# Sliding-window attention by groups of 64 queries with one window of 128 keys each, values copied on chip

## The chip, the cores and the metric

One core of one Trainium2 chip. The metric is the device time of one execution in microseconds. Experiments e2 to e5 ran on one chip and e6 to e8 on another, each set with the kernel before in the same rounds: it took 341.51 us (median) with the first set and 340.94 with the second, at best 340.80 and 340.67. Engine names are the profile's: PE is TensorE's matmul, PEld its weight load, DVE is VectorE, ACT is ScalarE, POOL is GpSimd, SP is SyncE.

## The reference, cut to what matters

```python
# q, k, v: (8 batches, 8 heads, 576 positions, 64)
scores = q @ k.T / 8                       # masked: 0 <= i - j < 64
attn = softmax(scores)                     # each query sees at most 64 keys
x = (attn @ v) -> (4608 tokens, 512)
out = (relu(x @ w_gate) * (x @ w_val)) @ w_out      # d_ff = 1536
```

## The kernel before

The attention is done in 24 units of 192 queries (all heads), three for each batch. Two units make a tile of 384 tokens, whose FFN follows: 96 `h` matmuls over gate and value, then 36 `op` matmuls. (`h` is the hidden layer, `g_sb` the product of its two halves, `op` the output; `st` are the scores, `p` their exp.) One instruction stream for PE weaves the two together. A small Python scheduler decides the order while the program is built: every piece of work advances a model clock by its estimated length, and attention steps are queued at planned times T on that clock.

```python
def at(self, t, fn): heapq.heappush(self.heap, (t, self.n, fn)); ...
def pop(self):
    _, _, fn = heapq.heappop(self.heap)
    self.clock += fn() or 0.0              # a step returns its estimate in us
def advance(self, t):                      # called between FFN matmul groups
    while self.heap and self.heap[0][0] <= max(t, self.clock): self.pop()
...
def u_st(u, hhs=(0, 1)):                   # scores, keys on partitions
    for hh in hhs:
        for w in range(2):                 # two windows of 128 keys x 128 queries
            for dh in range(2):
                for g in range(G):         # four row groups side by side
                    nc.tensor.matmul(d["st"][hh][g][:, c:c + 128], kT[...128 keys], qT[...128 queries], ...)
    return 0.65
def u_pv_wide(u):                          # units 2 to 23
    for c in (0, 2, 1, 3):
        for e in range(2):
            for w in range(2):
                nc.tensor.matmul(d["pv"][...][..., 64 * w:64 * w + 128], v16[:, w, ...], d["p"][...128], ...)
    return 0.9
...
def plan_unit(u, T, exp=0.8, mask=1.5, pv=3.9, ...):
    if u > 5: W.at(T - 17, lambda: v_load(u))
    W.at(T, lambda: u_st(u))
    ...                                    # exp and mask of the four head groups, copy, sum, norm
    W.at(T + pv, lambda: u_pv(u))
...
for t in range(3, NU // 2):                # two units a tile
    ...                                    # the batch's k and q
    plan_unit(2 * t, T + ...)
    plan_unit(2 * t + 1, T + 13.2, ...)
    T += 26.525
...
for t in range(2, NU // 2):
    ready(2 * t + 2)                       # emit everything up to this tile's xt
    hidden(t, 0, TT)                       # 96 h matmuls
    output(t)                              # 36 op matmuls
```

The end of a unit is a chain on DVE: PV result, four transposes of the sums (`sT`), reciprocal (`rT`), transpose back (`rs`), the product `xt`. The FFN of a tile waits for its second unit's `xt`. A new batch's k and q are transposed on DVE too (`kT`, `qT`).

The softmax here doesn't subtract the row's maximum and nothing guards it: scores larger than these inputs give would overflow.

## Time and profile before

| | before |
|---|---|
| median (all runs at first) | 340.94 us (340.88 to 341.48) |
| profiled span, granted clock | 339.0 us, 0.999 |
| PE busy | 98% |
| DVE, ACT busy | 74%, 55% |

A group's line reads: source line, engine, operation, written tile <- read tiles, shapes, count, then busy us and mean ns of one, then the idle time just before and who ended it. A line of the chain of waits reads: start, length, what.

### The profile page before, as it was taken

The numbers are of one execution on the slowest core, as the hardware profiler recorded it, in microseconds if no ns is written. First come the engines' busy times: TensorE is split into PE (matmuls) and PEld (weight loads), VectorE is DVE, ScalarE is ACT, GpSimd is POOL, SyncE is SP. The second block draws the span as 40 slices with busy tenths as digits, with TensorE's granted clock in tenths as the row PEclk, the third lists the DMA queues.
The fourth block names the chain that finished last, engine by engine and source line by source line (L and its number), as shares of the span: only waits on it lengthen the run. The fifth ranks groups of instructions, "written<-read, shape, count | busy, mean of one in ns | idle before, by whom it ended". The sixth has DMA issues, their size and how long they took to land.

```text
span 339.0 us, 7368 instructions
## 1 busy us (share of the span) xinstructions
PE 331.4 (98%) x2954; PEld 201.0 (59%) x2954; DVE 251.9 (74%) x452; ACT 186.1 (55%) x383; POOL 65.6 (19%) x99
## 2 busy tenths in 40 slices
PE   8899999999999999999999999999999999999996
PEld 4576496856546646646556555555655664664653
DVE  5777969997989748797798783888878963974430
ACT  4657166746736637638546556565565663663322
POOL 8723421411204004021021310420120200000000
PEclk9999999999999999999999999999999999999999
DMA  8999999980374854962251951972324402001002
GB/s 216 177 207 196 203 189 170 134 132 7 20 123 31 143 85 54 151 93 41 16 64 64 151 75 63 121 87 90 24 19 106 34 2 93 2 2 63 31 2 94
DMA packets 59666, 30.29 MB, mean 89 GB/s; under 512 B 46064, under 2 KB 51056, under 8 KB 59632
## 3 DMA queue, kind: packets, MB, share of 16 engines
q0 software_dynamic: 53872, 19.21, 51.8%
q1 hardware_dynamic: 5616, 10.55, 8.5%
q8 instruction: 23, 0.38, 0.5%
q14 instruction: 11, 0.09, 0.1%
q10 hardware_dynamic: 144, 0.07, 0.1%
HBM read 39.58 MB, written 9.44 MB: 145 GB/s over the span
## 4 chain that ended last, share of the span: by engine, by line
PE 85%; DVE 10%; issue 3%; ACT 1%; ACTq 0%
PE h L412 50%; PE op L426 21%; PE pv L305 6%; PE st L246 3%; DVE sT L335 3%; PE st L213 2%; DVE g_sb L400 2%; DVE qT L184 1%; DVE xt L350 1%; DVE p L266 1%; DVE kT L184 1%; PE op L458 1%; ACT p L260 1%; DVE rs L344 1%; PE st L206 1%
## 5 line engine op out<-in xcount | busy, mean ns | idle before, releaser
L412 PE MATMUL h<-xt,wg 128*128 128x384 f16 (+1 forms) x640 | 116.5, 310 | 0.7 <-DVE xt L350 0.7
L412 PE MATMUL h<-xt,wv 128*128 128x384 f16 (+1 forms) x640 | 116.4, 310 | 0.0
L400 DVE TENSOR_TENSOR g_sb<-r_sb,h 128x384 f16<-128x384 f32 x144 | 78.1, 549 | 50.3 <-PE h L412 48.3
L397 ACT ACTIVATE r_sb<-h 128x384 f32<-128x384 f32 x144 | 71.1, 495 | 52.0 <-PE h L412 43.4
L426 PE MATMUL op<-wo,g_sb 128*128 128x512 f16 x420 | 93.0, 379 | 0.0
L412 PEld LDWEIGHTS <-wg 128*128 128x128 f16 x640 | 59.3, 98 | 34.7 <-DVE xt L350 1.4
L412 PEld LDWEIGHTS <-wv 128*128 128x128 f16 x640 | 59.7, 98 | 31.6
L192 POOL DMA_DIRECT2D v<-in_v_dram x48 | 40.4, 846 | 185.7 <-PE pv L305 166.3
L426 PEld LDWEIGHTS <-g_sb 128*128 128x128 f16 x420 | 40.9, 98 | 47.9 <-DVE g_sb L400 0.4
L335 DVE STREAM_TRANSPOSE sT<-pv 64x384 f32<-64x384 f32 x88 | 51.1, 580 | 11.3 <-PE pv L305 9.8
L260 ACT ACTIVATE p<-st 128x512 f16<-128x512 f32 x92 | 49.9, 606 | 10.4 <-PE st L246 10.3
L433 ACT COPY o_sb<-op 128x512 f32<-128x512 f32 x35 | 20.5, 585 | 60.6 <-PE op L426 60.5
L323 ACT COPY xv<-pv 64x384 f32<-64x384 f32 x88 | 41.6, 473 | 17.6 <-DVE sT L335 8.5
L266 DVE TENSOR_TENSOR p<-p,mask 128x512 f16<-128x512 f16 x88 | 34.4, 419 | 7.0 <-ACT p L260 6.3
L305 PE MATMUL pv<-p,v 128*128 128x128 f16 x352 | 24.1, 219 | 0.4 <-DVE p L266 0.3
L344 DVE STREAM_TRANSPOSE rs<-rT 128x768 f32<-128x768 f32 x24 | 23.5, 978 | 0.8
L305 PEld LDWEIGHTS <-v 128*128 128x128 f16 x352 | 21.6, 98 | 3.7 <-issue 0.6
L350 DVE TENSOR_TENSOR xt<-xv,rs 128x768 f16<-128x768 f32 x24 | 22.7, 947 | 0.8
L184 DVE STREAM_TRANSPOSE kT<-k 128x576 f32<-128x576 f32 (+1 forms) x18 | 20.0, 1119 | 2.1 <-ACT k L177 1.7
L184 DVE STREAM_TRANSPOSE qT<-q 128x576 f32<-128x576 f32 x16 | 19.0, 1239 | 1.2 <-DMA q<-in_q_dram 1.2
L246 PEld LDWEIGHTS <-kT 32*128 32x128 f16 x768 | 11.4, 92 | 8.3 <-issue 8.3
L246 PE MATMUL st<-qT,kT 32*128 32x128 f16 x768 | 15.9, 215 | 0.4 <-DVE qT L184 0.4
(46 smaller groups left out, 79.0 us busy)
## 6 DMA issues: line engine op xcount, KB each, us to landing
out_dram<-o_sb SPq DMA_DIRECT2D x35, 256.0 KB, 2.0
v<-in_v_dram POOLq DMA_DIRECT2D x38, 128.0 KB, 4.1
q<-in_q_dram POOLq DMA_DIRECT2D x16, 288.0 KB, 8.4
k<-in_k_dram POOLq DMA_DIRECT2D x14, 288.0 KB, 6.7
wg<-in_moe_w_gate_dram POOLq DMA_DIRECT2D x3, 512.0 KB, 11.1
wv<-in_moe_w_val_dram POOLq DMA_DIRECT2D x3, 512.0 KB, 12.9
wo<-in_moe_w_out_dram POOLq DMA_DIRECT2D x3, 512.0 KB, 16.3
k<-in_k_dram SPq DMA_DIRECT2D x2, 576.0 KB, 3.9
```

The costliest lines, as they stand in the source:

```text
L184: nc.vector.transpose(dst.rearrange("p (i j) -> p j i", i=32)[:, j0:j1], src[:, j0:j1])
L192: nc.gpsimd.dma_start(v16[p0:128, w, :, 0:64], v[b, :, k0 + p0:k0 + 128].rearrange("h p d -> p h d"))
L246: nc.tensor.matmul(d["st"][hh][g][:, c:c + 128], kT[rows, hh, ks + 128 * w:ks + 128 * w + 128, dh], qT[rows, hh, ks + 64 * w:ks + 64 * w + ...
L260: nc.scalar.activation(d["p"][g].rearrange("p h c -> p (h c)"), d["st"][0][g], ACT.Exp, scale=scale)
L266: nc.vector.tensor_tensor(p, p, mask.rearrange("p w c -> p (w c)")[:, None, :].to_broadcast([128, 2, 256]), MUL)
L305: nc.tensor.matmul(d["pv"][c % 2][:, c // 2, e, 64 * w:64 * w + 128], v16[:, w, 128 * h - 64 * e:128 * h - 64 * e + 128], d["p"][h % G][:, ...
L323: nc.scalar.copy(d["xs"][rows, n::2], d["pv"][n][rows, :, e, 0:U])
L335: nc.vector.transpose(to[64 * e:64 * e + 64, half::2], d["pv"][half][64 - 64 * e:128 - 64 * e, :, e, 0:U])
L397: nc.scalar.activation(part(r_sb), part(h1), ACT.Relu)
L400: nc.vector.tensor_tensor(g_sb[:, f:f + w, c0:c1], part(r_sb), part(h2), MUL)
L412: nc.tensor.matmul(h[:, b * n:b * n + n], wt[:, c, (f + b) * 128:(f + b) * 128 + 128], xt[:, c, c0:c1], start=(c == 0), stop=(c == NC - 1))
L426: nc.tensor.matmul(op, g_sb[:, f, bass.ds(sub * 128, 128)], wo[:, f], start=(f == 0), stop=(f == NF - 1))
```

## The change

It means to compute little more than a group of 64 queries can see: for scores, exp, mask and PV, three groups of 64 queries by 128 keys a unit instead of two of 128 by 128, a quarter fewer columns everywhere. The three windows overlap by half, so v is loaded into the upper 64 partitions alone (`v_load`, not shown) and the lower 64 are filled by copies on DVE. In the cut below, comments after `#` are notes on the cut.

```diff
-            for w in range(2):
+            for w in range(UB):                                   # scores; UB = 3
...
-                            d["st"][hh][g][:, c:c + 128],
-                            kT[rows, hh, ks + 128 * w:ks + 128 * w + 128, dh],
-                            qT[rows, hh, ks + 64 * w:ks + 64 * w + 128, dh],
+                            d["st"][hh][g][:, c:c + 64],
+                            kT[rows, hh, ks + 64 * w:ks + 64 * w + 128, dh],
+                            qT[rows, hh, ks + 64 * w:ks + 64 * w + 64, dh],
...
-        return 0.65
+        return 0.55
...                                          # exp and mask: 512 -> 384 columns
+    def v_low(u):
+        uu = u % UB
+        if uu > 0:
+            nc.vector.tensor_copy(v16s[uu][0:64, 0, :, 0:64], v16s[uu - 1][64:128, UB - 1, :, 0:64])
+        nc.vector.tensor_copy(v16s[uu][0:64, 1:UB, :, 0:64], v16s[uu][64:128, 0:UB - 1, :, 0:64])
...                                          # PV, wide form
-                for w in range(2):
+                for w in range(UB):
...
-                        d["p"][h % G][:, h // G, 128 * w:128 * w + 128],
+                        d["p"][h % G][:, h // G, 64 * w:64 * w + 64],
...
-        return 0.9
+        return 0.7
...
+        W.at(T + 1.4, lambda: v_low(u))
```

More of the change, by code (lines that the diff above doesn't have):

```diff
@@ L85 @@
     kTs = [persist.tile([128, 2, 64 + S, 2], FP16, name=f"kT{i}") for i in range(2)]
-    v16s = [persist.tile([128, 2, H, 128], FP16, name=f"v16_{i}") for i in range(UB)]
+    v16s = [persist.tile([128, UB, H, 128], FP16, name=f"v16_{i}") for i in range(UB)]
     ones0 = consts.tile([128, 64], FP16)
     ones = consts.tile([128, 64], FP16)
-    mask = consts.tile([128, 2, 128], FP16)
-    bias = consts.tile([128, 2, 128], FP16)
+    mask = consts.tile([128, 64], FP16)
+    bias = consts.tile([128, 64], FP16)
     ident = consts.tile([128, 128], FP16)
@@ L98, in bands @@
         nc.gpsimd.memset(ident, 1.0)
-        for band, lo, hi in ((ident, 0, 0), (mask[:, 0], 64, -1), (mask[:, 1], 0, 63)):
+        for band, lo, hi in ((ident, 0, 0), (mask, 64, -1)):
+            n = band.shape[1]
             nc.gpsimd.affine_select(
                 out=band, in_=band, compare_op=mybir.AluOpType.is_ge, fill=0.0,
-                base=lo, pattern=[[1, 128]], channel_multiplier=-1,
+                base=lo, pattern=[[1, n]], channel_multiplier=-1,
             )
@@ L105, in bands @@
                 out=band, in_=band, compare_op=mybir.AluOpType.is_ge, fill=0.0,
-                base=hi, pattern=[[-1, 128]], channel_multiplier=1,
+                base=hi, pattern=[[-1, n]], channel_multiplier=1,
             )
@@ L115, in v_ones @@
         eng.memset(v16s[i][64 if i == 0 else 0:, 0, :, 64:128], 1.0)
-        eng.memset(v16s[i][:, 1, :, 64:128], 1.0)
+        for w in range(1, UB):
+            eng.memset(v16s[i][:, w, :, 64:128], 1.0)
     def k_zeros():
@@ L187, in v_load @@
         b, uu = divmod(u, UB)
-        v16 = v16s[uu]
-        for w in range(2):
-            k0 = U * uu - 64 + 128 * w
-            p0 = 64 if w == 0 and (uu == 0 or u < UB) else 0
-            nc.gpsimd.dma_start(v16[p0:128, w, :, 0:64], v[b, :, k0 + p0:k0 + 128].rearrange("h p d -> p h d"))
-    def v_before(u):
-        nc.vector.tensor_copy(v16s[u % UB][0:64, 0, :, 0:64], v16s[u % UB - 1][64:128, 1, :, 0:64])
+        for w in range(UB):
+            k0 = U * uu + 64 * w
+            nc.gpsimd.dma_start(v16s[uu][64:128, w, :, 0:64], v[b, :, k0:k0 + 64].rearrange("h p d -> p h d"))
+    def v_low(u):
[3 more added lines that the diff above has]
+        nc.vector.tensor_copy(v16s[uu][0:64, 1:UB, :, 0:64], v16s[uu][64:128, 0:UB - 1, :, 0:64])
     def u_bias(u, gs=range(G)):
@@ L204, in u_bias @@
         for to in d["st"][0] + d["st"][1] if u == 0 else [d["st"][0][g] for g in gs]:
-            n = to.shape[1] // 256
-            nc.tensor.matmul(to.rearrange("p (h c) -> p h c", h=n), ident,
-                             bias.rearrange("p w c -> p (w c)")[:, None, :].to_broadcast([128, n, 256]),
+            n = 1 if u == 0 else 2
+            nc.tensor.matmul(to[:, 0:n * U].rearrange("p (n c) -> p n c", c=64), ident,
+                             bias[:, None, :].to_broadcast([128, n * UB, 64]),
                              start=True, stop=False, skip_group_check=True)
@@ L240, in u_st @@
         for hh in hhs:
-            for w in range(2):
-                c = 256 * (hh if u else 0) + 128 * w
+            for w in range(UB):
+                c = U * (hh if u else 0) + 64 * w
                 for dh in range(2):
@@ L257, in u_exp @@
         if not hh:
-            d["p"][g] = a_p.tile([128, 2, 256], FP16, name="p")
+            d["p"][g] = a_p.tile([128, 2, U], FP16, name="p")
         if hh is None:
-            nc.scalar.activation(d["p"][g].rearrange("p h c -> p (h c)"), d["st"][0][g], ACT.Exp, scale=scale)
+            nc.scalar.activation(d["p"][g].rearrange("p h c -> p (h c)"), d["st"][0][g][:, 0:2 * U], ACT.Exp, scale=scale)
         else:
-            nc.scalar.activation(d["p"][g][:, hh], d["st"][hh][g][:, 0:256], ACT.Exp, scale=scale)
+            nc.scalar.activation(d["p"][g][:, hh], d["st"][hh][g][:, 0:U], ACT.Exp, scale=scale)
     def u_mask(u, g):
         p = units[u]["p"][g]
-        nc.vector.tensor_tensor(
-            p, p, mask.rearrange("p w c -> p (w c)")[:, None, :].to_broadcast([128, 2, 256]), MUL)
+        p = p.rearrange("p h (w c) -> p (h w) c", w=UB)
+        nc.vector.tensor_tensor(p, p, mask[:, None, :].to_broadcast([128, 2 * UB, 64]), MUL)
     def u_pv(u, cs=(0, 2, 1, 3)):
@@ L282, in u_pv @@
         for c in cs:
-            for s in range(2):
-                for w in range(2):
-                    for e in range(2):
-                        h = 2 * c + e
-                        nc.tensor.matmul(
-                            d["pv"][c][64 * e:64 * e + 64, s, 64 * w:64 * w + 128],
-                            v16[:, w, h, 0:64] if s == 0
-                            else (ones0 if u % UB == 0 and w == 0 else ones),
-                            d["p"][h % G][:, h // G, 128 * w:128 * w + 128],
-                            start=(s == 0 and w == 0), stop=(s == 1 and w == 1),
-                            skip_group_check=True)
+            for w in range(UB):
+                for e in range(2):
+                    h = 2 * c + e
+                    nc.tensor.matmul(
+                        d["pv"][c][64 * e:64 * e + 64, 0, 64 * w:64 * w + 64],
+                        v16[:, w, h, 0:64], d["p"][h % G][:, h // G, 64 * w:64 * w + 64],
+                        start=(w == 0), stop=True, skip_group_check=True)
+            for w0, w1, one in ((0, 1, ones0), (1, UB, ones)) if u % UB == 0 else ((0, UB, ones),):
+                for e in range(2):
+                    h = 2 * c + e
+                    nc.tensor.matmul(
+                        d["pv"][c][64 * e:64 * e + 64, 1, 64 * w0:64 * w1],
+                        one, d["p"][h % G][:, h // G, 64 * w0:64 * w1],
+                        start=False, stop=True, skip_group_check=True)
         return 1.2
@@ L303, in u_pv_wide @@
                 h = 2 * c + e
-                for w in range(2):
+                for w in range(UB):
                     nc.tensor.matmul(
-                        d["pv"][c % 2][:, c // 2, e, 64 * w:64 * w + 128],
+                        d["pv"][c % 2][:, c // 2, e, 64 * w:64 * w + 64],
                         v16[:, w, 128 * h - 64 * e:128 * h - 64 * e + 128],
-                        d["p"][h % G][:, h // G, 128 * w:128 * w + 128],
-                        start=(e == 0 and w == 0), stop=(e == 1 and w == 1),
+                        d["p"][h % G][:, h // G, 64 * w:64 * w + 64],
+                        start=(e == 0 and w == 0), stop=True,
                         skip_group_check=True)
-        return 0.9
+        return 0.7
     def u_copy(u, n):
@@ L539 @@
         W.at(11.9, lambda: u_sum(0, 0))
-        W.at(12.0, lambda: v_before(1))
+        W.at(11.2, lambda: v_low(0))
+        W.at(12.15, lambda: v_low(1))
         W.at(12.1, lambda: u_sum(0, 1))
@@ L551 @@
         W.at(21.0, lambda: v_ones(2, nc.vector))
-        W.at(18.0, lambda: v_before(2))
         W.at(21.0, lambda: v_ones(0, nc.vector))
```

## The prediction

It reckons a matmul of N columns at N/2.4 + 2.5 ns, a form that fits the starts in the trace of the kernel before: 55.7 ns apart at N=128, 162.5 at 384, 215.8 at 512.

> **What bounds the kernel now.** I read the page first, then the chain that ended last, then the VectorE and GpSimd timelines around the attention steps. From the page:
>
> ```profile
> PE 331.4 (98%) x2954; PEld 201.0 (59%) x2954; DVE 251.9 (74%) x452; ACT 186.1 (55%) x383; POOL 65.6 (19%) x99
> L246 PE MATMUL st<-qT,kT 32*128 32x128 f16 x768 | 15.9, 215 | 0.4 <-DVE qT L184 0.4
> L305 PE MATMUL pv<-p,v 128*128 128x128 f16 x352 | 24.1, 219 | 0.4 <-DVE p L266 0.3
> L266 DVE TENSOR_TENSOR p<-p,mask 128x512 f16<-128x512 f16 x88 | 34.4, 419 | 7.0 <-ACT p L260 6.3
> L260 ACT ACTIVATE p<-st 128x512 f16<-128x512 f32 x92 | 49.9, 606 | 10.4 <-PE st L246 10.3
> ```
>
> PE is full; DVE and ACT are not. So only PE time, or a new wait of PE, moves the end. The chain of waits of one steady stretch, in order of time (start, length, what):
>
> ```profile
> 116.67 0.89 PE pv L305 x16
> 117.56 0.65 PE h L412 x4
> 118.21 7.77 PE op L426 x36
> 125.98 0.65 PE h L412 x4
> ```
>
> One PV step is 16 matmuls in 0.89 us (55.7 ns each); 4 h matmuls (N=384) take 0.65; 36 output matmuls (N=512) take 7.77, so 0.2158 each. After the PV of a tile's second unit, PE has 8.42 us of other work (4 h + 36 op) before the next tile's first h matmul (125.98) needs the normalised `xt`. Under that cushion runs the DVE chain, here of the last unit (PV ends 303.90), then of a unit that also transposes the next k:
>
> ```profile
> 303.93 1.18 DVE L335 STREAM_TRANSPOSE sT<-pv 64x384 f32<-64x384 f32 x2 [0.56 <-PE pv L305]
> 305.14 0.55 DVE L400 TENSOR_TENSOR g_sb<-r_sb,h 128x384 f16<-128x384 f32 x1
> 305.73 1.18 DVE L335 STREAM_TRANSPOSE sT<-pv 64x384 f32<-64x384 f32 x2
> 306.94 0.30 DVE L342 RECIPROCAL rT<-sT 128x24 f32<-128x24 f32 x1
> 307.27 0.98 DVE L344 STREAM_TRANSPOSE rs<-rT 128x768 f32<-128x768 f32 x1
> 308.36 0.96 DVE L350 TENSOR_TENSOR xt<-xv,rs 128x768 f16<-128x768 f32 x1
> ```
> ```profile
> 147.11 1.26 DVE L184 STREAM_TRANSPOSE kT<-k 128x576 f32<-128x576 f32 x1
> 148.21 0.24 DVE L342 RECIPROCAL rT<-sT 128x24 f32<-128x24 f32 x1
> 148.49 0.98 DVE L344 STREAM_TRANSPOSE rs<-rT 128x768 f32<-128x768 f32 x1
> 149.39 1.22 DVE L184 STREAM_TRANSPOSE kT<-k 128x576 f32<-128x576 f32 x1
> 150.45 0.94 DVE L350 TENSOR_TENSOR xt<-xv,rs 128x768 f16<-128x768 f32 x1
> ```
>
> Without the g_sb between the two sT pairs, PV's end to `xt` is 0.04 + 2×1.21 (sT pairs, start to next start) + 0.33 + 1.09 + 0.96 + 0.05 (to PE's restart) = **4.9 us**; with two kT inside it is 0.04 + 2.42 + 4.28 (147.11 to 151.39) + 0.05 = **6.8 us**. Both are below 8.42: `xt` is ready 2 to 3 us early today.
>
> [...] The trace agrees at N=128 (55.7), 384 (0.65/4 = 162.5) and 512 (215.8); at N=64 it would be 29.2, which no run shows yet. [...] in this trace the loads hide behind a 55.7 ns matmul, and whether they hide behind 29 ns is open. [...]
>
> **The change, part by part.**
> PV: 16 matmuls of N=128 become 24 of N=64: 0.891 to 24×29.2 = 0.701 us, −0.19. Scores: 32 matmuls, four row groups at a time (8 sets, 0.46 us between the trace's starts, 57.7 ns a set), become 12 sets of about 30.9: 0.37, −0.09. For 22 steady units: 22×0.28 = **−6.2 us** of PE work. About 0.18 us of drain around each score step stays.
> ACT: exp 512 to 384 columns, −0.107 us each[...]: off the path. DVE: mask 512 to 384[...], four per unit; new copies of v to the lower partitions, 290 ns for 512 elements (the v copy's row in the profile) [...]. DVE has room for that in the steady part, not at the start (below). GpSimd: three half-height v loads per unit for two; not the bound.
>
> **The plan's clock, which I take as the decisive part.** The Python scheduler places attention steps at planned times T, and each emitted step advances its clock by its estimate: per tile 24×4×391/2400 = 15.64 (h), 36×519/2400 = 7.785 (op), 2×0.65 (scores), 2×0.9 (PV) = 26.525, exactly the `T += 26.525` in the code. The change lowers the estimates to 0.55 and 0.7 (25.925) but leaves T's step. So each tile's attention slips 0.6 us later relative to its FFN work, and it accumulates. The built order on TensorE confirms it. Before, 4 h + 36 op follow each second PV up to the next tile's h. After, only op matmuls do, for tiles 2 to 11: 21, 32, 29, 26, 23, 20, 18, 15, 12, 9. The cushion shrinks from 8.42 to 9×0.2158 = 1.94 us. The changed DVE order has no g_sb in these chains; units 7, 11, 13, 17, 19 (tiles 3, 5, 6, 8, 9) have the two kT. PE's wait per tile, chain less cushion:
> - tile 2: 4.9−4.53 = 0.4; tiles 3, 4: none
> - tile 5: 6.8−5.61 = 1.2; tile 6: 6.8−4.96 = 1.8; tile 7: 4.9−4.32 = 0.6
> - tile 8: 6.8−3.88 = 2.9; tile 9: 6.8−3.24 = 3.6; tile 10: 4.9−2.59 = 2.3; tile 11: 4.9−1.94 = 3.0
> Together **+15.8 us**.
>
> **A second new wait, at unit 2.** GpSimd issues unit 2's v loads at 12.53:
>
> ```profile
> 12.53 1.59 POOL L192 DMA_DIRECT2D v<-in_v_dram  x2
> 27.32 0.43 DVE L266 TENSOR_TENSOR p<-p,mask 128x512 f16<-128x512 f16 x1 [0.57 <-ACT p L260]
> 30.01 0.89 PE pv L305 x16
> ```
>
> The DMA view gives 16.5 to 16.8 us to landing, behind the weights, so about 29.3 to 29.8: just in time for PV at 30.0. The changed DVE queue has the v copies ahead of unit 2's first mask, so masks that ran from 27.3 wait until about 29.5. Then copy to 30.0, and four masks (0.3) with three g_sb (0.5) between: 32.7; the PV half that needs the last mask ends at about 33.1 instead of 30.9: **+2.2 us**.
>
> Smaller: where DVE is already dense before 92 us (units 3, 4, 5, 7; PE waits there 0.3 to 0.5 us at a time), the copies and the shifted order add about +1.3 together; PE's two 0.35 us waits for qT before the scores of units 12 and 18 disappear, −0.7, since those steps fall later after h; start-up about +0.3 (two copies before unit 0's reciprocal, shorter exps against them).
> Sum: 340.9 − 6.2 + 15.8 + 2.2 + 1.3 − 0.7 + 0.3 = **353.6 us**.
>
> **The rivals.**
> (a) The intended gain: PE does 6.2 us less and nothing new waits, 334.5. For it: PE is 98% busy. Against: the emitted order leaves 1.9 us of work over a 4.9 us chain, and arithmetic of durations already in the trace closes no gap of that size.
> (b) N=64 is no faster, because loads or issue bind at about 40 ns: PV 24×40 = 0.96 instead of 0.70, 22×0.26 = +5.7, about 359. For it: loads and matmuls grow by half in number. Against: at the start of a score step two loads into the same row group begin 14 ns apart in the trace.
> (c) DVE becomes the bound everywhere through the v copies. Against: it is busy 19.1 of the 26.5 us from 99.5 to 126 (the view by windows); only the first 90 us are dense. I give it 1.3 us above.
> (d) The stalls of 3 us and more let the clock drop[...]. Before, PE idled 0.9 us in a row (PV of unit 1, waiting for exp) without it; I leave it in the upper tail.
>
> **Range and chances.** The slip term is arithmetic on the built order and recorded durations; its error is perhaps 2 us. Unit 2 may cost 0 to 4, N=64 −1 to +6, the clock 0 to +3. I say **353.6, with 348.5 to 359.5**. Slower by over 2% begins at 347.8. Chances: faster 0.03, same 0.06, slower 0.91.
>
> **What would show it.** Right: PV with 24 matmuls in about 0.70 us and score sets about 31 ns apart; PE waiting at h for DVE xt at tiles 5 to 11, most at 9 and 11 (3 us), in all 14 to 18 us; DVE waiting for the v DMA near 27 to 29.5 us; clock about 1. Wrong: PE busy still 98% and a shorter span (then the slip does not bind, the step I would have to give up); PV at 0.9 us or more (rival b); waits at PV for masks throughout (rival c); a clock below 0.98 (rival d).

## The result, and the profile after

The changed kernel took **363.04 us** (median of 4, 360.76 to 364.26), the kernel before 340.93 in the same rounds: ratio 1.063 (95% interval 1.059 to 1.068). A ratio here is the mean time of one kernel's fast runs over that of the other's of the same rounds, so not quite the ratio of the medians. It is slower, by more than I said. The profiled execution is the fastest of the four, 360.76, with a span of 358.9.

From the page of the changed kernel: busy time, the slices of PE and of its clock, and the two groups that the change reshaped:

```profile
PE 331.9 (92%) x3522; PEld 198.5 (55%) x3522; DVE 261.3 (73%) x493; ACT 176.6 (49%) x383; POOL 73.9 (21%) x121
...
PE   8698999999999999989979999969969997996995
...
PEclk9989999999999999999999999999998998999899
...
L311 PE MATMUL pv<-p,v 128*128 128x64 f16 x528 | 20.3, 193 | 1.9 <-DVE p L270 1.8
...
L249 PE MATMUL st<-qT,kT 32*128 32x64 f16 x1152 | 13.6, 189 | 1.0 <-DVE qT L186 0.8
```

PE was 98% busy and is now 92%. The attention's matmuls did get cheaper: PV 24.1 to 20.3 us, scores 15.9 to 13.6. But holes (slices at 6 or 7) stand in the second half of the PE row, where one slice is 9 us, and the clock row dips to 8 in or just after the last three of them. The view of waits, PE only, names the holes; its columns are total us, times, longest:

```profile
PE h L419 <- DVE xt L356: 16.7, 10, 3.6
PE pv L311 <- DVE p L270: 1.8, 4, 0.5
```

Before, the first of these was 0.7 us in all. One of them, tile 9, in the chain of waits (its sT steps are cut):

```profile
258.64 3.34 PE op L433 x15
261.98 0.72 PE pv L311 x24
...
265.14 1.26 DVE kT L186
...
266.52 0.98 DVE rs L350
...
268.49 0.95 DVE xt L356
...
269.48 4.67 PE h L419 x19
```

The 24 PV matmuls take 0.70 us (0.72 with the hand-over), 29 ns each. Of the 36 op matmuls, 21 (6 + 15) now come before the PV and only 15 after, 3.2 us of work above a DVE chain of 6.8. PE stands from 265.8 to 269.5. Then the first 19 h take 4.67 us, where 162.5 ns each would be 3.1. The view by windows shows why; it gives the window, its length, the busy time of PE, PEld, DVE, ACT and POOL (and counts), then the granted clock, DMA share and GB/s:

```profile
265.60:269.00 3.40, 0.32 (x2) 0.04 (x1) 3.37 (x5) 0.59 (x1) 0.00 (x0) 1.00 0.84 122
269.00:272.40 3.40, 2.92 (x10) 1.41 (x10) 1.67 (x3) 0.49 (x1) 0.00 (x0) 0.50 0.00 0
272.40:275.80 3.40, 3.40 (x23) 2.04 (x22) 2.57 (x4) 1.07 (x3) 0.00 (x0) 1.00 0.00 0
```

An idle stretch of 3.4 us, then 3.4 us at half clock, in which PE began 10 matmuls; then 23 at full clock. Such a window at half clock came after tiles 9, 10 and 11 and once at the start (16.4 us).

At unit 2, the DVE timeline shows the copy that waits for its v load, with the first mask behind it:

```profile
28.52 0.29 DVE L198 COPY v<-v 64x512 f16<-64x512 f16 x1
29.81 0.42 DVE L199 COPY v<-v 64x1024 f16<-64x1024 f16 x1 [1.00 <-DMA v<-in_v_dram]
30.27 0.36 DVE L270 TENSOR_TENSOR p<-p,mask 128x384 f16<-128x384 f16 x1
```

### The profile page after: what moved, and what is told of

Its sections match the earlier page's. It is cut to its first block, busy times and chain, and to the rows that moved or that the text cites. A ratio compares the mean times of both kernels' runs of the same rounds, so it can differ in the third digit from the quotient of the medians.

```text
span 358.9 us, 8610 instructions
## 1 busy us (share of the span) xinstructions
PE 331.9 (92%) x3522; PEld 198.5 (55%) x3522; DVE 261.3 (73%) x493; ACT 176.6 (49%) x383; POOL 73.9 (21%) x121
## 4 chain that ended last, share of the span: by engine, by line
PE 73%; DVE 15%; DMA 4%; POOL 3%; issue 3%; ACT 1%; DVEq 0%; ACTq 0%; POOLq 0%
PE h L419 49%; PE op L433 16%; DVE sT L341 5%; DMA v<-in_v_dram 4%; PE pv L311 4%; PE st L249 3%; DVE xt L356 2%; DVE rs L350 2%; DVE kT L186 2%; POOL v L192 1%; DVE g_sb L407 1%; DVE p L270 1%; PE op L465 1%; POOL wv L151 1%; POOL wg L151 1%
## 5 line engine op out<-in xcount | busy, mean ns | idle before, releaser
L419 PE MATMUL h<-xt,wg 128*128 128x384 f16 (+1 forms) x640 | 120.5, 318 | 17.6 <-DVE xt L356 16.7
L419 PE MATMUL h<-xt,wv 128*128 128x384 f16 (+1 forms) x640 | 118.9, 315 | 0.0
L433 PE MATMUL op<-wo,g_sb 128*128 128x512 f16 x420 | 95.5, 379 | 0.1
L419 PEld LDWEIGHTS <-wg 128*128 128x128 f16 x640 | 61.1, 100 | 54.6 <-issue 18.4
L192 POOL DMA_DIRECT2D v<-in_v_dram x72 | 49.3, 694 | 198.3 <-PE pv L311 84.4
L263 ACT ACTIVATE p<-st 128x384 f16<-128x384 f32 x92 | 39.6, 493 | 16.5 <-PE st L249 16.5
L270 DVE TENSOR_TENSOR p<-p,mask 128x384 f16<-128x384 f16 x88 | 28.8, 355 | 8.8 <-ACT p L263 8.1
L311 PEld LDWEIGHTS <-v 128*128 128x128 f16 x528 | 18.9, 98 | 6.8 <-issue 2.5
L311 PE MATMUL pv<-p,v 128*128 128x64 f16 x528 | 20.3, 193 | 1.9 <-DVE p L270 1.8
L249 PE MATMUL st<-qT,kT 32*128 32x64 f16 x1152 | 13.6, 189 | 1.0 <-DVE qT L186 0.8
```

The source lines that it names most:

```text
L192: nc.gpsimd.dma_start(v16s[uu][64:128, w, :, 0:64], v[b, :, k0:k0 + 64].rearrange("h p d -> p h d"))
L249: nc.tensor.matmul(d["st"][hh][g][:, c:c + 64], kT[rows, hh, ks + 64 * w:ks + 64 * w + 128, dh], qT[rows, hh, ks + 64 * w:ks + 64 * w + 64 ...
L263: nc.scalar.activation(d["p"][g].rearrange("p h c -> p (h c)"), d["st"][0][g][:, 0:2 * U], ACT.Exp, scale=scale)
L270: nc.vector.tensor_tensor(p, p, mask[:, None, :].to_broadcast([128, 2 * UB, 64]), MUL)
L311: nc.tensor.matmul(d["pv"][c % 2][:, c // 2, e, 64 * w:64 * w + 64], v16[:, w, 128 * h - 64 * e:128 * h - 64 * e + 128], d["p"][h % G][:, ...
L419: nc.tensor.matmul(h[:, b * n:b * n + n], wt[:, c, (f + b) * 128:(f + b) * 128 + 128], xt[:, c, c0:c1], start=(c == 0), stop=(c == NC - 1))
```

## The experiments

**Theory A** is the prediction's: the estimates were lowered and the plan's step was not, so attention slips 0.6 us a tile and PE runs into the DVE chain. **Theory B**: the new matmul forms or the copies make the waits. On the clock, **C**: PE's idle stretches lower it and this costs time; **D**: the drop costs nothing, as PE is waiting anyway. The expectations of e2 and e8 give the order on PE as it was built. Unit ends below are start times of a unit's last PV matmul in the trace.

**e2: only the slip, in the kernel before.**

```diff
-        return 0.65
+        return 0.55
-        return 0.9
+        return 0.7
```

> The kernel before, with only the two estimates that the attention steps return lowered to 0.55 and 0.7 (scores, values, copies unchanged). Its TensorE order has the same cushions of output matmuls as the changed kernel: 21, 32, 29, 26, 23, 20, 18, 15, 12, 9 for tiles 2 to 11. Theory A (the slip of the plan makes the waits, whatever the tiles of the matmuls are): 340.9 + 16.5 (the waits measured at h of tiles 5 to 11 in the changed kernel) + about 5 to 7 for half-clock windows = 360 to 365 us, clock near 0.975. Theory B (the new matmul forms or the on-chip v copies make the waits): 341 us, clock 0.999.

Measured: 364.88 us (361.75 to 365.53) against 341.51, ratio 1.066 (1.061 to 1.072). From PE's waits and the page:

```profile
PE h L412 <- DVE xt L350: 16.6, 10, 3.5
```
```profile
PEclk9999999999999999999999999989998998998899
```

Two numbers in Python, which change no matmul and only the order, reproduce a loss as large as the whole change's: 16.6 us of waits in place of 16.7, and dips of the clock of the same kind, though not at the same places: five half-clock windows after tiles 8 to 11 and none at the start, where the changed kernel has three and one. B is refuted as the main cause.

**e3: the change without the slip.**

```diff
-        return 0.55
+        return 0.65
-        return 0.7
+        return 0.9
```

> The changed kernel, with only the two estimates put back to 0.65 and 0.9. Theory A: the cushion is 4 h + 36 op again, no PE wait at h of tiles 3 to 11; 340.9 - 6.2 (PE work) + 1.0 (start-up) + 1.6 (unit 2 behind its v load) + about 1 (units 4, 5, 7) = 338 to 340 us; clock 0.99 or more. Theory B: the waits stay, above 355 us.

Measured: 340.15 us (340.13 to 340.31), ratio 0.996 (0.993 to 0.998), just above the 338 to 340 expected. PE's waits:

```profile
PE h L419 <- DVE g_sb L407: 2.4, 2, 1.8
PE pv L311 <- DVE p L270: 2.2, 5, 0.7
...
PE h L419 <- DVE xt L356: 0.5, 2, 0.3
```

16.7 us became 0.5. The kernel is the change with its intended effect, and barely faster than before. From unit 8's to unit 23's PV it takes 194.83 us where before took 198.96: 0.275 us a unit, times 22 the −6.1 us that PE was to save. What it gains there it had lost earlier: unit 7's PV ends at 94.52, before at 90.83. Unit 2's copy and the DVE-bound units 4, 5 and 7 are in that; e5 and e6 take them apart. The profiled execution also has a half-clock window at 15.5 us, but it cost little: it took 340.31, and the three executions at clock 1.000 took 340.13 to 340.15.

**e4: the changed kernel kept warm in its waits.**

```diff
+    FILL = {5: 5, 6: 8, 7: 2, 8: 13, 9: 16, 10: 10, 11: 13}
...
             ready(2 * t + 2)
+            if t in FILL:
+                heat(FILL[t], op_tile())     # matmuls on zeros, never read
             hidden(t, 0, TT)
```

> The changed kernel with dummy matmuls on zeros (N=512, 5, 8, 2, 13, 16, 10, 13 of them) put where TensorE waits before the first h of tiles 5 to 11, so that it is busy but does nothing useful and cannot start earlier. Theory C (idle TensorE of 2.5 to 3.7 us lets the clock drop to half for 3.4 us after each such wait, which my prediction left out of its sum): clock 0.99 or more and 5 to 8 us less than the changed kernel, 355 to 358 us. Rival D (the drop costs nothing, as TensorE is waiting anyway): the time stays at 361 to 364.

Measured: 356.38 us (356.07 to 357.49), ratio 1.044 (1.041 to 1.047), where the changed kernel had 1.063. The clock rose from 0.979 to 0.995; its row, and the same tile 9:

```profile
PEclk9998999999999999999999999999999999999999
```

```profile
260.17 3.34 PE op L434 x15
263.51 0.72 PE pv L311 x24
...
270.01 0.95 DVE xt L356
...
271.01 6.66 PE h L420 x40
```

The chain is as long as ever (7.5 us from PV's start to the end of `xt` in both), so the wait is untouched, but the 40 h after it now take 6.66 us, 166 ns each: full clock. In the changed kernel the same 40 took 8.09. C holds: the drops cost about 6.7 us (363.04 − 356.38; the two ratios differ by 0.019, which is 6.6), and useless work during a wait gave them back. Trace against trace (the changed kernel's profile is its fastest execution, this one its slowest) it is 4.8: from unit 7's PV to PE's last matmul 254.3 us here, 259.1 in the changed kernel, and its three half-clock windows after tiles 9 to 11 are worth about 4.7 together. One half-clock window, at 31.9 us, is left, behind a wait of 2.3 us at unit 2.

**e5: unit 2's v copy behind its masks**, on top of e3.

```diff
-        W.at(T + 1.4, lambda: v_low(u))
+        W.at(T + (3.5 if u == 2 else 1.4), lambda: v_low(u))
```

> e3_est_back with the v copy of unit 2 alone queued behind that unit's four masks (planned at T+3.5, not T+1.4). Theory E (VectorE stands still behind unit 2's v load and holds masks and g_sb back): 1.0 to 1.7 us less than e3_est_back, and TensorE's waits of 1.0 and 0.6 us near 30 to 33 us go down to a few tenths. Rival (the DMA's landing binds, wherever the copy stands): no difference over 0.4 us.

Measured: 339.04 us (338.57 to 339.28), ratio 0.992 (0.989 to 0.996), 1.1 less than e3. Unit 2's PV ends at 31.95 instead of 33.45. E holds. e5 reaches unit 2's scores 0.2 us later than e3 (26.65, 26.43), so the move is worth 1.7 us by there. PE's waits fall from 2.0 and 0.6 us to 0.56 and 0.31; what is left is PV waiting for the copies themselves, as PE's view of waits names them:

```profile
PE pv L311 <- DVE v L198: 0.4, 1, 0.4
```

**e6: four more copies moved to idle places** (unit 1's between unit 0's sT pairs, units 4 and 7's before the sT of the unit ahead, unit 5's on ACT), on top of e5.

```diff
-        W.at(T + (3.5 if u == 2 else 1.4), lambda: v_low(u))
+        at, how = {2: (T + 3.5, nc.vector.tensor_copy), 4: (46.3, nc.vector.tensor_copy), 5: (54.6, nc.scalar.copy),
+                   7: (77.1, nc.vector.tensor_copy)}.get(u, (T + 1.4, nc.vector.tensor_copy))
+        W.at(at, lambda: v_low(u, how))
...
-        W.at(12.15, lambda: v_low(1))
+        W.at(12.05, lambda: v_low(1))
```

> e5_vlow2 with four v copies moved to where their engine waits for TensorE or is idle: unit 1's between unit 0's two pairs of sT, units 4 and 7's before the sT of the unit ahead, unit 5's on ScalarE. Theory F (in the first 92 us VectorE's chains are the bound, so each 0.5 us of copies taken off them comes back): 0.9 (unit 4) + 0.5 (unit 5) + 0.5 (unit 7) + 0.3 (start) less than e5_vlow2, 336.5 to 337.5 us. Rival (they are bound by masks and exp and the copies are hidden): within 0.4 us of e5_vlow2's 339.0.

Measured: **335.84 us** (335.72 to 336.55), ratio 0.985 (0.984 to 0.987), below the 336.5 to 337.5 expected, 3.2 less than e5 by the medians and 2.5 by the ratios (another chip), and faster than both kernels, though still "same" by the 2% rule, as e3, e5, e7 and e8 are. Its page:

```profile
PE 324.9 (97%) x3522; PEld 196.2 (59%) x3522; DVE 259.0 (78%) x491; ACT 177.6 (53%) x385; POOL 74.2 (22%) x121
```

PE is busy 324.9 us, 6.5 less than before. Unit by unit, from the end of the PV ahead: unit 4 8.16 us for 9.04 in e5, unit 5 8.05 for 8.81, unit 7 8.15 for 8.93, and unit 2 ends 0.5 earlier: 2.9 together, where the two traces differ by 3.0. F holds; the stretch is bound by DVE there.

**e7: v by DMA instead of copies, units 6 to 23**, on top of e5.

```diff
-            nc.gpsimd.dma_start(v16s[uu][64:128, w, :, 0:64], v[b, :, k0:k0 + 64]...)
+            p0 = 64 if u < 2 * UB or k0 == 0 else 0
+            nc.gpsimd.dma_start(v16s[uu][p0:128, w, :, 0:64], v[b, :, k0 + p0 - 64:k0 + 64]...)
...                                           # v_low only for u < 6
```

> e5_vlow2 with the on-chip copy undone for units 6 to 23: their v comes by DMA for all 128 partitions, no v copy on VectorE. Theory G (the copies cost nothing in the steady part, where VectorE has time over; only unit 7's is on a path): 0.3 to 0.7 us less than e5_vlow2, all of it before 95 us, and the same pace from unit 8 to 23 (208.5 us). Rival (the copies slow the steady part too): 1.5 us or more less.

Measured: 337.79 us (337.20 to 338.01), ratio 0.991 (0.989 to 0.992), 1.25 less than e5 by the medians. I had expected 0.3 to 0.7, a miss, though by the two ratios it is 0.65. In the traces, which differ by 1.2, unit 7 gave 0.8 (8.14 us for 8.93). Another 0.37 is there by unit 2, before the edited code runs; its cause is open. From unit 8 to 23 the pace is 194.81 against 194.83 (the expectation's 208.5 counts from unit 7's end: 208.42 against 208.44): the copies cost nothing where DVE has time, and G holds in that.

**e8: the slip mended from the other end**, in the changed kernel with e5's copy.

```diff
-            T += 26.525
+            T += 25.925
```

> The changed kernel (lowered estimates kept) with the plan's step lowered with them, T += 25.925, and unit 2's v copy behind its masks as in e5_vlow2. 32 output matmuls (6.9 us) stay between each second PV and the next h from tile 3 on, just over the 6.8 us chain. Theory A (only the accumulation hurts): no PE wait over 0.2 us at h of tiles 3 to 11, within 1.5 us of e5_vlow2: 338 to 340.5 us. Against it: 345 us or more.

Measured: 340.41 us (340.00 to 340.80), ratio 0.998 (0.997 to 0.9995). PE waits 0.29 to 0.30 us at h of tiles 3, 5, 6, 8 and 9, the five with kT in their chain, instead of up to 3.7. I had said no wait over 0.2 us: the chain of 6.8 is 7.2 here (6.9 of op plus 0.3), and was 6.96 in the changed kernel. A holds, by a second mend. Of the 1.4 us above e5 (by the medians) the five waits are 1.5, and the qT waits that it lacks take 0.8 off. The rest is not taken apart; a half-clock window at 16.5 us is in it, worth at most part of it: the execution at clock 1.000 took 340.00, the other three 340.27 to 340.80.

## Why the prediction was right or wrong

The direction and the mechanism were right, the size was not: 353.6 was said, 348.5 to 359.5 as the range, 363.04 measured. Taking each matmul's start distance in the trace less N/2.4 + 2.5 ns as waiting (at N=64 too the form fits: 29 ns measured), the profiled execution gives, term by term (the ends of PE's work are 355.01 and 335.44 us, so 19.6 to explain):

| term of the sum | said | measured |
|---|---|---|
| PE work saved, units 2 to 23 | −6.2 | −6.1 |
| waits for `xt`, tiles 2 to 11 | +15.8 | +16.9 |
| unit 2 behind its v load | +2.2 | +1.65 |
| units 3, 4, 5, 7 | +1.3 | +2.1 |
| qT waits at units 12, 18 | −0.7 | −0.7 |
| start-up without the clock | +0.3 | −0.3 |
| half-clock windows | 0 in the sum | +6.1 |

- **PE work** (right). PV's 24 matmuls are 29 ns apart, score sets about 30: "at N=64 it would be 29.2" and "about 30.9". The starts of PV's loads are 29 ns apart too (median), though the record of a single load is 98 ns long, so here the loads hide behind 29 ns as well. Rival (b), whose 40 ns was an assumption, is out.
- **The plan's clock** (right, and the main thing). Tile by tile, from 5 to 11, the prediction said 1.2, 1.8, 0.6, 2.9, 3.6, 2.3, 3.0; measured were 1.36, 2.00, 0.74, 3.07, 3.72, 2.46, 3.11. e2, e3 and e8 show that the slip alone makes these waits, and that either mend removes nearly all. One reading in the prediction is loose: by its own figures `xt` was ready 1.6 to 3.5 us early, not 2 to 3.
- **Unit 2** (right in mechanism, a little too large). The copy stood 1.0 us for the DMA, as described; masks and g_sb then ran faster than I reckoned.
- **Units 3, 4, 5, 7** (right in mechanism, too small). DVE's busy time grew by 9.4 us (251.9 to 261.3), 0.39 a unit; that this is the missing 0.8 us is not shown, and the +1.3 was an estimate. The single sizes: 431 ns for the 1024-element copy and 286 for the 512-element one (290 said), masks 64 ns shorter (419 to 355), exps 113 (606 to 493; 107 said, and the kernel before has 606 at 512 columns and 390 at 256, which is 108 for 128).
- **Rival (d), the clock: the step that failed.** The prediction put it so: "The stalls of 3 us and more let the clock drop", then "I leave it in the upper tail", and in the range, "the clock 0 to +3". I had a list with waits of 2.9, 3.6, 2.3 and 3.0 us beside it, and still added nothing to the sum. The runs show four half-clock windows of 3.41 us, from 16.4, 269.0, 299.7 and 330.4 us, in which the h matmuls start 320 ns apart at N=384 (162.5 at full clock) and, in the first, 160 at N=192 (82.5). The waits before the last three, at tiles 9, 10 and 11, were 3.72, 2.46 and 3.11 us. The wait of 3.07 us at tile 8 was followed by no drop, where in e2 that of 3.06 us was; why is not shown. The windows are worth 1.67 us of PE time each after tiles 10 and 11, 1.42 after tile 9, where PE idled in part of the window, and 1.3 at the start, 6.1 in all; the clock was 0.979, just under the 0.98 that the prediction named as the sign of this rival. e4 tests the windows after the tiles: it gave back 4.8 us by the traces and 6.7 by the medians. The one at the start was not tested, and e3 suggests that it moves the end by less. With all four the sum would have been 359.7, against 360.76 of the profiled run.
- **Open.** Three of the four executions are 2.3 to 3.5 us over the profiled one, two of them at a clock of 0.970 to 0.971, which fits two more windows by an estimate (0.0085 of 361 us is 3.1, two windows at 1.4 to 1.7 are 2.8 to 3.4); one is at 0.979, which doesn't. Why the number of half-clock windows differs between executions, and why the profiled ones of this kernel, e3 and e8 have one at the start and those of the other kernels none, is not shown.

## What to carry to other kernels

Where a program is ordered by a model clock, an estimate is part of the schedule: change it and every planned time that was added up from it has to follow, or the order drifts by a constant a round until a cushion is gone. When a change is to make PE wait, list the waits, and ask of each what the clock did after it as well as how long it was: here seven of the eight waits at tiles 8 to 11 of the changed kernel and e2 (2.46 to 3.72 us in the first, up to 3.5 in the second) were followed by 3.41 us at half clock, worth 1.42 to 1.67 us each in the changed kernel, and filling the waits with dummy matmuls (e4) gave 4.8 to 6.7 us back. A gain of 2% on the bounding engine (6.1 us of PE work here) can be largely eaten by a few added copies at the one place where another engine is the bound (moving five of them took the ratio from e3's 0.996 to e6's 0.985), so place small side work where its engine already waits.
